# Chunked attention ahead of a routed expert layer: where the first turned queries and second turned keys are put

## The chip, the cores and the metric

The kernel runs on one core of a Trainium2 chip. The metric is device time in microseconds (us) of one execution. Before the change three executions took 534.76, 535.52 and 537.1 us, a median of 535.52 us. One more execution was taken with the hardware profiler; it is the one that all rows below come from.

The core has five engines that run side by side, each with its own queue of instructions: TensorE (PE; its weight loads are shown as PEld), VectorE (DVE), ScalarE (ACT), GpSimd (POOL) and SyncE (SP), which here only issues transfers. An engine stands at an instruction until the semaphores that it waits for have been raised; all that stands behind it on that engine waits too.

## What is computed

```python
# attention: batch 4, 8 heads, 768 tokens of 64 numbers, 8 memory keys and values per head
for c in range(S // 32):                      # chunks of 32 queries
    q_c   = q[:, :, 32*c : 32*c + 32]
    k_ctx = k[:, :, max(0, 32*c - 16) : min(S, 32*c + 40)]
    k_full, v_full = concat(mem_k, k_ctx), concat(mem_v, v_ctx)
    a = softmax(q_c @ k_full.T / 8)
    out[:, :, 32*c : 32*c + 32] = a @ v_full
# routed layer: 3072 tokens of 512 numbers, 8 experts, one expert per token
logits = x @ w_gate
e = argmax(logits);  gate = softmax(logits)[e]
y = gate * (relu(x @ w1[e]) @ w2[e])
```

All is float32. The two stages follow each other in one kernel: the attention's output rows are labelled with their expert, scattered to an array in device memory by expert, fetched back expert by expert, multiplied, and scattered to the output.

## The kernel before, in words

**Tiling of the attention.** There are 32 blocks of 96 queries (`NB`), 8 to each of the 4 batches. Two blocks in a row share one load of queries and one of keys ("super block", 16 of them, index j). `load_q(j)` and `load_k(j)` bring 384 KB each: 96 partitions, of which each holds a pair of neighbouring tokens for 8 heads. The first super block of a batch has the 8 memory keys besides (4 more partitions). `load_v(i)` brings the values of one block in three transfers into one of 6 buffers.

**Turning.** Scores need queries and keys with the 64 numbers of a head along the partitions. `turned_heads` (L616) takes one half x of the heads of a super block, issues four transposes on TensorE into one PSUM tile of 128 x 4 x 96 (or 100 with the memory keys), and returns it. `turn_q(m)` (L622) turns half x of super block j, with m = 2j + x, and copies the result out in two instructions, by default on ScalarE, into `qT`. `turn_k(m)` (L629) does this for keys, by default on VectorE, into the turned keys `kT` of the batch; with memory keys it has two more, smaller copies (L649). In what follows k0, k1, k2, ... and q0, q1, ... are these calls by their m. So k0 and k1 are the two halves of the first load of keys, k2 and k3 those of the second, k4 and k5 those of the third.

**PSUM.** Eight banks are held as three pools: `ps_s`, two pairs of banks for scores; `ps_t`, two banks for turned tiles; `ps_o`, two banks for the values. A pool's tiles take turns, so a third tile of `ps_t` waits until the first has been read.

**The order.** All is issued in the order that the code gives (`manual_schedule`). After the first nine loads come k0, k1, q0, q1 (L1038 to L1041). Then the loop over blocks i (L1042): two or more loads for later blocks; `scores(i)` (L653), four matrix products into a pair of banks and three exponentials on ScalarE into `ex`; for i = 0 alone k2 and k3 (L1048 to L1050), whose tiles come from `ps_t`; `turn_q(i + 2)`; the values of block i - 1 (L680), whose two halves are divided on VectorE; transposes and router products for earlier blocks; `turn_k(i + 4)`; routing work. A matrix product or a transpose in float32 shows as one or two records in the trace; `scores` has 8, a turn 4, `values` 16 for both halves.

The scores of block 0 read keys that k0 and k1 have turned; those of block 1 reach into keys of the second load, k2 and k3. The scores of blocks 2 and 3 need q2 and q3, and k4 and k5 besides at block 3.

**What waits for what at the start, in the code before.** q0 needs the load of queries, and the PSUM bank of k0 back, which VectorE's four copies give free; q1 needs that of k1, after ScalarE's four. The first scores need q0's copies (VectorE, L1040) and q1's (ScalarE, L1041). k2 and k3 take the two banks of `ps_t` again, VectorE copies both, and q2 and k4 take them after that.

After the attention comes the expert layer, which the change doesn't touch.

Of the kernel before, what the change touches and what calls it, by code (L numbers as in the profile page):

```python
# [10 lines left out]
F32 = mybir.dt.float32  # L11
# [8 lines left out]
B, H, S, D = 4, 8, 768, 64  # L20
# [48 lines left out]
PAIRS = QB  # L69
# [16 lines left out]
def window(qb):  # L86
    return min(max(PER * qb - LEFT, 0), KW - WIN)
# [417 lines left out]
def ordinary(ctx, tc, q, k, v, mem_k, mem_v, moe_w_gate, moe_w1, moe_w2, out, good):  # L505

    nc = tc.nc
# [7 lines left out]
    def turn(*args):  # L515
        i = nc.tensor.transpose(*args)  # L516
        cur["pe"] = i.ins.name
        return i

    def bc(ap, axis, n):  # L520
        shape = list(ap.shape)
        shape.insert(axis, n)
        idx = tuple([slice(None)] * axis + [None])
        return ap[idx].to_broadcast(shape)
# [13 lines left out]
    ps_s = actx.enter_context(tc.tile_pool(name="ps_s", bufs=2, space=PSUM))  # L538
    ps_t = actx.enter_context(tc.tile_pool(name="ps_t", bufs=2, space=PSUM))
    ps_o = actx.enter_context(tc.tile_pool(name="ps_o", bufs=2, space=PSUM))  # L540
# [47 lines left out]
    def load_runs(to, i, start, n, src, mem):  # L588

        for p, kind, r, n in runs(start, n):  # L590
            ap = (mem if kind == "mem" else src)[i // NQB, :, r : r + n].rearrange("h r d -> r h d")
            nc.sync.dma_start(to[p : p + n], ap)

    sbs = [dict() for _ in range(NSB)]
# [5 lines left out]
    def load_q(j):  # L600
        t = sbs[j]["qn"] = lpool.tile([PAIRS, H, 2 * D], F32, name="qn")
        nc.sync.dma_start(t, pairs(q, j))
        sbs[j]["qT"] = qTs[j % NQ]

    def load_k(j):
        b, s = divmod(j, NSB // B)
        t = sbs[j]["kn"] = lpool.tile([PAIRS + NMEM // 2, H, 2 * D], F32, name="kn")
        nc.sync.dma_start(t[0:PAIRS], pairs(k, j))
        if s == 0:
            nc.sync.dma_start(t[PAIRS:], mem_k[b].rearrange("h (p t) d -> p h (t d)", t=2))  # L610

    def load_v(i):
        st[i]["v"] = vs[i % NV]
        load_runs(st[i]["v"][:, :, 0:D], i, window(i % NQB), WIN, v, mem_v)

    def turned_heads(t, n, x):  # L616
        tt = ps_t.tile([128, H // 2, n], F32, tag="t", name="tqk")
        for a in range(H // 2):
            turn(tt[:, a], t[0:n, 2 * a + x], ident[0:n, 0:n])
        return tt  # L620

    def turn_q(m, copy=nc.scalar.copy):  # L622
        j, x = divmod(m, 2)
        tq = turned_heads(sbs[j]["qn"], PAIRS, x)
        to = sbs[j]["qT"][D * x : D * x + D, :, x].rearrange("d a (p t) -> d a p t", t=2)
        for t in range(2):
            copy(to[:, :, :, t], tq[D * t : D * t + D])  # L627

    def turn_k(m, copy=nc.vector.tensor_copy):  # L629
        j, x = divmod(m, 2)  # L630
        b, s = divmod(j, NSB // B)
        if s == 0 and x == 0:
            turned[b] = apool.tile([128, H // 2, KW], F32, name="kT")
        n = PAIRS + NMEM // 2 if s == 0 else PAIRS
        tk = turned_heads(sbs[j]["kn"], n, x)
        half = turned[b][D * x : D * x + D]
        for t in range(2):
            of = tk[D * t : D * t + D]
            to = half[:, :, 2 * PER * s + t : 2 * PER * s + 2 * PER]
            to = bass.AP(  # L640
                tensor=to.tensor,
                offset=to.offset,
                ap=[list(to.ap[0]), [KW, H // 2], [PER, 2], [QB // 2 + NMEM, 2], [2, QB // 4]],
            )
            i = copy(to, of[:, :, 0:PAIRS].rearrange("d a (y z p) -> d a y z p", y=2, z=2))  # L645
            keyed.setdefault((b, s), []).append(i.ins.name)
            if s == 0:
                to = half.rearrange("d a (y c) -> d a y c", y=NQB)[:, :, :, QB // 2 : QB // 2 + NMEM]
                copy(  # L649
                    to.rearrange("d a y (p t) -> d a y p t", t=2)[:, :, :, :, t], bc(of[:, :, PAIRS:], 2, NQB)  # L650
                )
# [177 lines left out]
    def routing(n, kinds="v"):  # L829
        while work and n and work[0][0] in kinds:  # L830
            kind, f = work.pop(0)
            f()
            n -= kind != "s"

    def hold_back():

        while work and work[0][0] == "s":
            spread.append(work.pop(0)[1])

    def scatter_some(n):  # L840
        while spread and n:
            spread.pop(0)()
            n -= 1

    def need(i, f, *lists):
        if 0 <= i < NB:
            f(i)
# [180 lines left out]
    with tc.manual_schedule():  # L1028
        load_k(0)
        load_q(0)  # L1030
        load_k(1)
        load_q(1)
        load_v(0)
        load_k(2)
        load_v(1)
        load_q(2)
        load_v(2)
        turn_k(0)  # L1038
        turn_k(1, nc.scalar.copy)
        turn_q(0, nc.vector.tensor_copy)  # L1040
        turn_q(1)  # L1041
        for i in range(NB):  # L1042
            if i // 2 + 3 < NSB:
                (load_k, load_q)[i % 2](i // 2 + 3)
            need(i + 3, load_v)
            scores(i)
            scatter_some(1)
            if i == 0:  # L1048
                turn_k(2)
                turn_k(3)  # L1050
            need(i + 2, turn_q)
            banks = [ps_o.tile([128, 512], F32, tag="o", name="o") for _ in range(2)]
            cur["bank"] = banks[0]
            if i <= 23:
                routing(1, "p")
            if i >= 1:
                values(i - 1, 0, banks[0])
            routing(5 if i > 23 else 3)
            need(i - 2, turn_xb)
            late = logits(i - 3, banks[1]) if i >= 3 else None  # L1060
            if i >= 1:
                values(i - 1, 1, banks[1])
            if late:
                nc.vector.tensor_copy(*late)
            if i > 23:
                routing(1, "p")
            scatter_some(1)
            need(i + 4, turn_k)
            routing(6 if i > 23 else 5)
            hold_back()  # L1070
            for g in range(len(GROUPS)):
                if i - 3 == GROUPS[g][1] - 1:
                    work.extend(routed(g))
            if i == 24:
                fetch_w(0, 4)
            if i >= 24:
                fetch_piece(1)
                fetch_piece(1)
            if len(scatters) >= EARLY and "early" not in cur:
                cur["early"] = i  # L1080
                early_count(banks[0])
                early_gather()

        early_rows()
        n = NB

        def bank_pair():
            banks = [ps_o.tile([128, 512], F32, tag="o", name="o") for _ in range(2)]
            cur["bank"] = banks[0]
            return banks  # L1090

        room_for_x()
        banks = bank_pair()
        values(n - 1, 0, banks[0])
        scatter_some(1)
        turn_xb(n - 2)
        late = logits(n - 3, banks[1])
        values(n - 1, 1, banks[1])  # L1100
        scatter_some(1)
        nc.vector.tensor_copy(*late)
        routing(99, "v")
        fetch_w(1, 1)
        fetch_piece(99)
        do_early(1)
        banks = bank_pair()
        late = logits(n - 2, banks[1])
        nc.vector.tensor_copy(*late)
        do_early(1)  # L1110
        turn_xb(n - 1)
        scatter_some(1)
        do_early(1)
        routing(1, "p")
        routing(99, "v")
        hold_back()
        banks = bank_pair()
        late = logits(n - 1, banks[1])
        nc.vector.tensor_copy(*late)
        work.extend(routed(len(GROUPS) - 1))  # L1120
        routing(99)
        check_sums()
        do_early(2)
        scatter_some(1)
        routing(1, "p")
        routing(99, "v")
        hold_back()
        do_early(1)
        scatter_some(1)
        count_up()  # L1130
        fetch_x(0)
        first_sums()
        while spread:
            do_early(1)
            scatter_some(1)
        index = [nc.tensor.value_load(cases[0:1, e : e + 1], min_val=0, max_val=len(ARMS) - 1) for e in range(E)]
        rv = nc.values_load(good[0:1, 0:1], min_val=0, max_val=1)
        tc.switch_hint({mybir.EngineType.PE: index[0]}, len(ARMS), "expert0")
        nc.tensor.addr_align(PAGE, 0, 0)
        do_early(len(early_ops))  # L1140
# [470 lines left out]
```

## Time and profile before

| | us |
|---|---|
| median of three executions | 535.52 |
| the profiled execution | 532.34 |
| its span, first to last instruction | 530.6 |
| TensorE busy within the span | 507.7 |
| VectorE busy | 300.0 |
| ScalarE busy | 245.7 |
| GpSimd busy | 156.0 |

The rows of a profile's group list give a line of the code, the engine, the operation, out<-in by the names of tiles, the count, the busy time and the mean of one in ns, and the idle time ahead of it with what ended most of that. The chain is the path of work that ended last, followed back from the last instruction; it can also be listed in order of time, as start, length, engine, tile, line and count. In the list of one line's instructions the three numbers are the shortest, the median and the longest duration in ns.

In the page's 40 slices TensorE is busy 90% or more in all but the first, one in the middle and the last. The transfer engines are busy 80% or more in the first twelve, at 154 to 344 GB/s. Over the first 40 us they moved 6.62 MB, at a mean of 165 GB/s.

### The profile page before, as it was taken

The page shows a single profiled execution, that of the slowest core. Times are in us where ns is not written, and L with a number is a line of the kernel's source. Part 1 is how long each engine was busy: PE and PEld are TensorE (multiplying, and loading weights), DVE is VectorE, ACT ScalarE, POOL GpSimd, SP SyncE. Part 2 cuts the span into 40 slices and gives each one's busy share as a digit, 9 for nine tenths or more (in the row PEclk, how much of TensorE's full clock was granted, in tenths as well). Part 3 has the DMA queues.
Part 4 walks back from the last instruction along what each step waited for, and adds up shares of the span by engine and source line. Part 5 has one row for each costly group of instructions (what it writes and reads, how often), then busy time and mean ns, then how long its engine had stood idle before and what let it go on. Part 6 is the DMA issues. An engine that isn't in the chain of part 4 may idle for free.

```text
span 530.6 us, 9604 instructions
## 1 busy us (share of the span) xinstructions
PE 507.7 (96%) x3666; PEld 475.7 (90%) x3666; DVE 300.0 (57%) x565; ACT 245.7 (46%) x445; POOL 156.0 (29%) x186
## 2 busy tenths in 40 slices
PE   3999999999999989999999999999999999999992
PEld 3899999999998569999999999977779999999991
DVE  3455656566555246878656557443625767864611
ACT  2466656556632136374553454344216637454311
POOL 2000131323373604354135054121312434412003
PEclk9999999999999999999999999999999999999997
DMA  9999999989982302446406335330505334200002
GB/s 171 154 171 181 182 224 200 224 201 344 303 308 73 88 15 81 172 172 229 176 15 221 96 128 208 102 134 30 195 18 199 139 125 182 81 15 13 1 1 84
DMA packets 81350, 75.02 MB, mean 141 GB/s; under 512 B 39543, under 2 KB 64375, under 8 KB 81281
## 3 DMA queue, kind: packets, MB, share of 16 engines
q1 hardware_dynamic: 71840, 54.60, 41.6%
q0 software_dynamic: 8768, 19.29, 11.0%
q8 instruction: 46, 0.75, 0.6%
q10 hardware_dynamic: 672, 0.18, 0.1%
q14 instruction: 24, 0.19, 0.1%
HBM read 66.13 MB, written 17.50 MB: 158 GB/s over the span
## 4 chain that ended last, share of the span: by engine, by line
PE 83%; issue 9%; DMA 3%; POOL 2%; ACT 1%; DVE 1%; POOLq 0%; ACTq 0%
PE sum_p L511 20%; PE sum_r L511 13%; PE sum_q L511 13%; PE o L511 11%; PE sc L511 8%; PE tqk L516 4%; PE sum_x L516 3%; PE ph L511 3%; PE py L511 3%; PE sum_q L516 2%; PE tx L516 2%; POOL out_dram L1276 2%; DMA xe<-x_dram,rows 1%; DMA x_dram<-xr,dest 1%; DMA kn<-in_k_dram 1%
## 5 line engine op out<-in xcount | busy, mean ns | idle before, releaser
L1276 POOL DMA_INDIRECT out_dram<-y,xe x42 | 51.0, 1214 | 177.1 <-PE sum_q L511 59.9
L1293 POOL DMA_INDIRECT xe<-x_dram,rows x35 | 50.7, 1448 | 49.8 <-PE sum_r L511 29.2
L676 ACT ACTIVATE ex<-sc,cst 128x256 f32<-128x256 f32 x96 | 38.5, 472 | 56.5 <-PE sc L511 56.5
L511 PE MATMUL o<-v,ex 128*96 128x65 f32 x512 | 54.5, 251 | 0.0
L1227 ACT COPY sum_r<-sum_p 128x640 f32<-128x640 f32 x48 | 32.5, 677 | 47.3 <-PE sum_p L511 47.2
L511 PE MATMUL sc<-qT,kT 128*128 128x192 f32 x256 | 50.6, 343 | 1.1 <-ACT qT L627 1.1
L511 PEld LDWEIGHTS o<-v,ex 128*96 128x96 f32 x512 | 49.4, 167 | 0.0
L511 PE MATMUL sum_p<-xsT,w 128*128 128x136 f32 (+6 forms) x256 | 47.6, 329 | 0.5
L511 PE MATMUL sum_r<-t,w 128*128 128x136 f32 (+6 forms) x256 | 45.8, 326 | 0.0
L511 PE MATMUL sum_p<-t,s 128*128 128x136 f32 (+6 forms) x256 | 45.6, 326 | 0.0
L801 POOL DMA_INDIRECT x_dram<-xr,dest x32 | 30.2, 944 | 52.5 <-PE tqk L516 21.3
L511 PE MATMUL sum_q<-t,s 128*128 128x136 f32 (+6 forms) x256 | 45.1, 324 | 0.0
L511 PEld LDWEIGHTS sc<-qT,kT 128*128 128x128 f32 x256 | 43.2, 199 | 1.4 <-issue 1.4
L511 PEld LDWEIGHTS sum_p<-xsT,w 128*128 128x128 f32 x256 | 39.7, 190 | 4.8 <-issue 2.1
L511 PE MATMUL sum_p<-h,w 128*128 128x136 f32 (+6 forms) x256 | 43.8, 324 | 0.0
L511 PEld LDWEIGHTS sum_p<-t,s 128*128 128x128 f32 x256 | 39.7, 190 | 2.6
L511 PEld LDWEIGHTS sum_r<-t,w 128*128 128x128 f32 x256 | 39.6, 190 | 2.6
L511 PEld LDWEIGHTS sum_q<-t,s 128*128 128x128 f32 x256 | 39.8, 190 | 2.3
L511 PEld LDWEIGHTS sum_p<-h,w 128*128 128x128 f32 x256 | 39.5, 190 | 2.3
L1224 DVE TENSOR_TENSOR h<-sum_p,kept 128x640 f32<-128x640 f32 x16 | 13.2, 824 | 48.4 <-ACT sum_r L1227 48.4
L645 DVE COPY kT<-tqk 64x384 f32<-64x384 f32 x62 | 34.3, 554 | 10.4 <-PE tqk L516 9.8
L690 DVE RECIPROCAL inv_all<-o 96x4 f32<-96x4 f32 x64 | 11.4, 179 | 48.0 <-PE o L511 47.7
(154 smaller groups left out, 916.9 us busy)
## 6 DMA issues: line engine op xcount, KB each, us to landing
w<-in_moe_w_dram SPq DMA_DIRECT2D x14, 2048.0 KB, 8.6
kn<-in_k_dram SPq DMA_DIRECT2D x16, 384.0 KB
qn<-in_q_dram SPq DMA_DIRECT2D x16, 384.0 KB
w<-in_moe_w_dram SPq DMA_DIRECT2D x8, 512.0 KB
v<-in_v_dram SPq DMA_DIRECT2D x24, 128.0 KB
v<-in_v_dram SPq DMA_DIRECT2D x24, 112.0 KB
v<-in_v_dram SPq DMA_DIRECT2D x8, 144.0 KB
v<-in_v_dram SPq DMA_DIRECT2D x8, 96.0 KB
```

The lines of the kernel that those rows point to most:

```text
L511: i = nc.tensor.matmul(*args, **more)
L516: i = nc.tensor.transpose(*args)
L645: i = copy(to, of[:, :, 0:PAIRS].rearrange("d a (y z p) -> d a y z p", y=2, z=2))
L676: nc.scalar.activation(ex4[:, :, :, sl], sc4[:, :, :, sl], AF.Exp, bias=mask[:, 3 * x + g : 3 * x + g + 1], scale=D**-0.5)
L690: nc.vector.reciprocal(inv, o[:, :, D])
L801: i = nc.gpsimd.indirect_dma_start(out=x_dram, out_offset=bass.IndirectOffsetOnAxis(ap=dest[:, t : t + 1], axis=0), in_=xr[:, t % NXR].bit ...
L1224: op(eng, one_op(lambda: engines[eng].tensor_tensor(out, a, b, op=how)), reads, writes)
L1227: op("ACT", one_op(lambda: nc.scalar.copy(to, of)), reads, writes)
L1276: return nc.gpsimd.indirect_dma_start(out=out, out_offset=bass.IndirectOffsetOnAxis(ap=which.bitcast(I32), axis=0), in_=y, in_offset=None, ...
L1293: return nc.gpsimd.indirect_dma_start(out=x[:, g].bitcast(I32), out_offset=None, in_=x_dram, in_offset=bass.IndirectOffsetOnAxis(ap=rows[: ...
```

## The change

Two tiles are taken from `ps_o` and one pair of banks from `ps_s` before the loop. q0 and q1 are turned into the first two, k2 and k3 into the two banks of the pair. k2 and k3 stand ahead of the loop now, after q1, and so ahead of the scores of block 0; k3 is copied by ScalarE and not by VectorE.

```diff
-    def turned_heads(t, n, x):
-        tt = ps_t.tile([128, H // 2, n], F32, tag="t", name="tqk")
+    def turned_heads(t, n, x, bank=None):
+        if bank is None:
+            tt = ps_t.tile([128, H // 2, n], F32, tag="t", name="tqk")
+        else:
+            tt = bank[:, 0 : H // 2 * n].rearrange("p (a n) -> p a n", a=H // 2)
...
+        first = [ps_o.tile([128, 512], F32, tag="o", name="o") for _ in range(2)]
+        second = ps_s.tile([128, 2, 512], F32, tag="s", name="sc")
         turn_k(0)
         turn_k(1, nc.scalar.copy)
-        turn_q(0, nc.vector.tensor_copy)
-        turn_q(1)
+        turn_q(0, nc.vector.tensor_copy, first[0])
+        turn_q(1, bank=first[1])
+        turn_k(2, bank=second[:, 0])
+        turn_k(3, nc.scalar.copy, second[:, 1])
         for i in range(NB):
...
             scores(i)
             scatter_some(1)
-            if i == 0:
-                turn_k(2)
-                turn_k(3)
             need(i + 2, turn_q)
```

`turn_q` and `turn_k` take the argument `bank` and hand it on to `turned_heads`.

More of the change, by code (lines that the diff above doesn't have):

```diff
@@ L620, in turned_heads, with turn_q @@
         return tt
-    def turn_q(m, copy=nc.scalar.copy):
+    def turn_q(m, copy=nc.scalar.copy, bank=None):
         j, x = divmod(m, 2)
-        tq = turned_heads(sbs[j]["qn"], PAIRS, x)
+        tq = turned_heads(sbs[j]["qn"], PAIRS, x, bank)
         to = sbs[j]["qT"][D * x : D * x + D, :, x].rearrange("d a (p t) -> d a p t", t=2)
@@ L627, in turn_q, with turn_k @@
             copy(to[:, :, :, t], tq[D * t : D * t + D])
-    def turn_k(m, copy=nc.vector.tensor_copy):
+    def turn_k(m, copy=nc.vector.tensor_copy, bank=None):
         j, x = divmod(m, 2)
@@ L634, in turn_k @@
         n = PAIRS + NMEM // 2 if s == 0 else PAIRS
-        tk = turned_heads(sbs[j]["kn"], n, x)
+        tk = turned_heads(sbs[j]["kn"], n, x, bank)
         half = turned[b][D * x : D * x + D]
```

## The prediction

> **What bounds the kernel now.** First the page's share of busy time and its chain of waits, which say that TensorE sets the end:
>
> ```profile
> PE 507.7 (96%) x3666; PEld 475.7 (90%) x3666; DVE 300.0 (57%) x565; ACT 245.7 (46%) x445; POOL 156.0 (29%) x186
> PE 83%; issue 9%; DMA 3%; POOL 2%; ACT 1%; DVE 1%; POOLq 0%; ACTq 0%
> ```
>
> So the change is worth what it does to TensorE's own line of work. That line has holes only at the start, so next the chain in order of time (start, length, what):
>
> ```profile
> 0.74 5.27 DMA kn<-in_k_dram
> ...
> 6.11 0.92 PE tqk L516 x4
> ...
> 8.68 1.53 PE tqk L516 x8
> ...
> 11.32 2.90 PE sc L511 x8
> 14.22 0.65 PE tqk L516 x4
> ...
> 16.05 0.55 DVE kT L645
> ...
> 16.61 0.57 DVE kT L645
> ...
> 17.28 0.87 PE tqk L516 x4
> 18.15 2.61 PE sc L511 x8
> ```
>
> From the first load TensorE turns k0 and k1, stands until 8.68, turns q0 and q1, stands until 11.32 for ScalarE's copies of q1, does the first scores, turns k2 and k3 (14.01 to 15.50), and then follows VectorE, whose four copies of k2 and k3 end at 17.18 and give free the banks of q2 (16.12) and of k4 (17.28). The second scores start at 17.94. From there TensorE has no hole until 27.08: third scores 23.61, one block each 4.35 us from 27.35 on.
>
> Third, the same instruction before and after some 22.75 us (four rows of lists by line: shortest, median, longest ns):
>
> ```profile
> L516 PE MATMUL tqk<-cst,kn x8: 367/367/368, 14.0 to 15.1; 96*128 96x96 f32 x8
> L511 PE MATMUL sc<-qT,kT x8: 527/527/581, 17.9 to 20.2; 128*128 128x192 f32 x8
> L511 PE MATMUL sc<-qT,kT x8: 326/326/355, 27.7 to 28.9; 128*128 128x192 f32 x8
> L516 PE MATMUL tqk<-cst,kn x8: 246/246/303, 23.3 to 27.7; 96*128 96x96 f32 x8
> ```
>
> Starts of the score records are 0.32 us apart before and 0.16 after, those of turns 0.16 and 0.08: TensorE runs at half its pace until 22.75, though the column of granted clock says 1.00 there. All of the change lies in the slow part.
>
> Fourth, when the loads land, by the trace's landing records: first keys 6.02, first queries 8.04, second keys 9.89, second queries 11.97, third keys 16.67, fourth keys 25.16. The load engines are saturated in this time (share 1.1 to 1.3 in each stretch of the first 40 us), and the change moves no load and no wait ahead of one that is late: the two loads that now wait for another turn (that of the second queries' successor, that of the second keys') are issued at over 21 us, long after those turns.
>
> **The change part by part.** What TensorE does is the same in count: no transpose, product or byte is added. VectorE gives two copies of 0.56 to ScalarE (0.50 each by its rows for k1, L645). What moves is waits.
>
> 1. q0 no longer needs k0's bank. Before, it went at 8.68, 0.09 after VectorE's last copy of k0 (8.59). Now its load is the bound: 8.04, plus the 0.09 that k0 needed after its own (6.02 to 6.11): 8.13, so 0.55 earlier. q0's copies start 0.91 later as before (8.68 to 9.59): 9.04 to 10.18 on VectorE. q1's on ScalarE start 1.55 after the first turn: 9.68 to 10.70 (1.02 for both, gap included).
> 2. k2 stands next: its load lands at 9.89, so 9.98 to 10.64 on TensorE (4 x 0.16). VectorE copies it 0.91 after the start, 10.89 to 12.01 (2 x 0.56).
> 3. k3 should follow at once. In the program built from the change it does not: its first transpose waits for VectorE's count, and the count it waits for is raised by the second copy of k2, though the two lie in two banks; they are one tile. So it goes at 12.01 + 0.09 = 12.10, done at 12.75. Queued behind it on TensorE are the first scores, which were ready at 10.79 (q1's copies). They start at 12.75 and not at 11.32: 1.43 late. Behind those, the exponentials of block 0 on ScalarE wait. ScalarE copies k3 in the hole ahead of them: 13.0 to 14.0.
> 4. After the first scores (2.69 from start to start of the next): 15.44. q2's turn has a free bank and its load: 15.44 to 16.08. k4 needs no copy now, its bank is long free, but the third keys land at 16.67: 16.76 to 17.42. Second scores: k3's copies 14.0, fine; they start at 17.42, against 17.94.
> 5. So the sum up to the second scores is -0.52 us: k2's and k3's copies (17.18) are taken off, and the third load of keys (16.67) takes their place. The 1.43 of step 3 costs nothing, because the hole ahead of 16.76 (0.68 of it) covers it; without that hole the second scores would be bound by 12.75 + 2.69 + 0.64 + 0.66 = 16.74, still earlier than before.
> 6. What is late next: the exponentials of block 0 go from 14.25 to 15.70, end 16.90, then q2's copies (1.0) until 17.9. Values of block 0 come at 20.67, q3's turn at 20.02 (needs q2's bank, 17.9): 3.8 and 2.1 us of cover. At 27.08 TensorE waits 0.27 for ScalarE's q copies, in step with the third scores, so this moves along. The fourth keys (25.16) have 2.2 of cover at 27.35.
>
> What the 0.52 are worth at the end depends on the moment when the pace doubles. If that stays at 22.75, TensorE has done 0.52 us of slow work more by then, which is 0.26 at full pace. If it moves along with the unbroken work (before: 17.28 to 22.75), it is 0.52. Ends of this unknown: -0.26 and -0.52; I take the middle, -0.4.
>
> [...]
>
> **The sum.** Profiled execution: 532.34 - 0.4 = 531.9 (span 530.2 of 530.6). The median of the runs is 3.2 above the profiled one; the same step on it: 535.52 - 0.4 = 535.1. That is 0.07%, and I call up to 0.5% (2.7 us) no change, about what a measurement of this kernel can tell: its three executions lie 2.3 apart.
>
> **The rivals.**
>
> *Full pace comes earlier, and this is worth more.* The stretch 12.10 to 16.08 has no hole now: 3.98 us. If that alone doubles the pace, from about 16: k4 16.76 to 17.10, second scores to 18.43, q3 18.77, values of block 0 to 20.1, third scores after ScalarE's q3 copies (exponentials 18.5 to 19.7, copies to 20.7) at 20.8 against 23.61: -2.8. Then the turn of the fourth keys would be due at 24.5, and they land at 25.16: only 27.35 - 25.25 = 2.1 is kept. 535.5 - 2.1 = 533.4. For it: the stretch is long. Against: before, 11.32 to 15.50 was longer (4.18) and did not do it. Loads cap it below 0.5%, so only with the spread of executions on top is it over the bound.
>
> [...]
>
> *The change doesn't do what it says: nothing is won.* Step 3 shows half of this: turns into the pair run one after the other. If the third keys land 0.5 later than in the profiled execution, k4 goes at 17.28 as before: 535.5.
>
> **How the numbers follow.** Forecast (0.1 to 0.5 us won) 0.60: 535.1, its own range 533.6 to 536.7 by the spread of the three executions. Nothing won 0.18: 535.5. Earlier full pace 0.13: 533.4. Later full pace 0.09: 539.5. The range goes from 532.6 (earlier pace, with some spread) to 537.6; beyond it lie most of the last case and tails of the others, under 2 in 10. Faster by over 0.5% (under 532.8): 0.16, half of the earlier pace and the low tail of the executions, of which the profiled one was already at 532.3. Slower by over 0.5% (over 538.2): 0.14, the later pace and the high tail. The rest, 0.70, within.
>
> **What would show it.** In the changed profile: q0's first transpose near 8.1; k3's behind a wait for VectorE's copy of k2, near 12.1; first scores near 12.75, later than before; k4's turn released by the third keys' landing near 16.75; second scores near 17.4. Wrong would be: k3 right behind k2 (step 3); a hole between 19.4 and 22.8 (slower rival); matrix products of 326 ns before 20 us (faster rival); or blocks after 30 us that no longer take 4.35, which no step of mine explains.

## The result, and the profile after

Twelve executions of the changed kernel gave a median of 536.36 us (532.67 to 538.51), twelve of the kernel before, run beside them, 536.40 (534.76 to 538.88). The ratio on record for the two sets, 0.9988, isn't that of the two medians (0.9999); its 95% interval is 0.9967 to 1.0009. By that interval the change is worth somewhere between 0.33% won and 0.09% lost: no difference that can be told. The forecast was 0.07% won.

The profiled execution after is the longer of the two profiles, 535.20 us with a span of 533.4, against 532.34 and 530.6. Its page:

```profile
span 533.4 us, 9602 instructions
...
PE 508.4 (95%) x3666; PEld 475.9 (89%) x3666; DVE 299.1 (56%) x563; ACT 246.5 (46%) x447; POOL 155.7 (29%) x186
...
PEclk9999999999988999999999999999999999999998
```

TensorE's work is the same 3666 records. What is new are the two 8s of the clock row, in the slices from 147 to 173 us (13.3 us each): TensorE ran for a while at half pace there.

The start, from the timeline (start, length, engine, line, operation, out<-in, count; in brackets the idle time ahead and what ended it):

```profile
8.22 1.54 PE L516 MATMUL o<-cst,qn 96*128 96x96 f32 x8 [0.58 <-DMA qn<-in_q_dram]
...
10.24 0.90 PE L516 MATMUL sc<-cst,kn 96*128 96x96 f32 x4 [0.48 <-DMA kn<-in_k_dram]
11.18 1.12 DVE L648 COPY kT<-sc 64x384 f32<-64x384 f32 x2 [0.90 <-PE sc L516]
...
12.36 0.90 PE L516 MATMUL sc<-cst,kn 96*128 96x96 f32 x4 [1.22 <-DVE kT L648]
...
13.06 2.82 PE L511 MATMUL sc<-qT,kT 128*128 128x192 f32 x8
...
15.67 0.79 PE L516 MATMUL tqk<-cst,qn 96*128 96x96 f32 x4
...
16.90 0.52 PE L516 MATMUL tqk<-cst,kn 96*128 96x96 f32 x4 [0.44 <-DMA kn<-in_k_dram]
...
17.26 1.49 PE L511 MATMUL sc<-qT,kT 128*128 128x192 f32 x8
```

The rows go q0 and q1, k2, its copies, k3, first scores, q2, k4, second scores. q0 is now released by its load, k3 by VectorE's copies of k2 (1.22 us of hole), k4 by the third keys. The second scores took 2.82 at their place before and take 1.49 here: in this execution the pace doubled at 16.27 by the trace's clock records, and not at 22.78. In all four profiles of kernels that keep the old start it doubled at 20.68 to 23.06; in the eight with the change or a part of it, and without products of ones at the start, it first did so at 13.76 to 20.45.

The chain in order of time shows what this ran into:

```profile
7.78 8.99 DMA kn<-in_k_dram
16.77 0.14 issue
16.90 0.33 PE tqk L516 x2
17.23 8.34 DMA kn<-in_k_dram
25.57 0.14 issue
25.71 0.52 PE tqk L516 x4
26.23 1.33 PE sc L511 x8
```

Two loads of keys in a row carry the chain from 7.78 to 25.57. TensorE waits 1.08 us for the second of them and then turns it at 25.71, 1.64 ahead of the 27.35 of the kernel before. From the same record counted along TensorE in both traces: it is 1.53 us ahead at 76 us and 1.81 ahead at 153. Then the lead is gone within one row. Before:

```profile
155.14 0.87 PE L511 MATMUL o<-v,ex 128*96 128x65 f32 x8
156.57 0.66 PE L516 MATMUL tx<-cst,xe 128*128 128x128 f32 x4 [0.56 <-DMA xe<-x_dram,rows]
...
158.99 1.99 PE L511 MATMUL ph<-x0T,w 128*128 128x256 f32 x8 [0.34 <-ACT x0T L993]
```

After:

```profile
153.12 0.39 PE L516 MATMUL tx<-cst,xr 96*128 96x96 f32 x2 [0.51 <-DVE xr L695]
...
153.96 0.87 PE L511 MATMUL o<-v,ex 128*96 128x65 f32 x8
156.48 1.12 PE L516 MATMUL tx<-cst,xe 128*128 128x128 f32 x4 [1.64 <-DMA xe<-x_dram,rows]
...
160.35 3.31 PE L511 MATMUL ph<-x0T,w 128*128 128x256 f32 x8
```

The row at 155.14 and 153.96 ends the attention's values. The next is the turn of the early rows: 256 rows of expert 0 that are fetched while the attention still runs. It starts at 156.5 in both, since its gather (the transfer that fetches these rows) lands then, at 156.52 and 156.43 by the chains, before and after:

```profile
150.16 6.36 DMA xe<-x_dram,rows
...
149.52 6.91 DMA xe<-x_dram,rows
```

The lead makes a hole of 1.64 us there and not 0.56, and one of 0.51 just ahead, at a turn of attention rows that waits for VectorE. Half pace follows (products of 128 x 256 take 3.31 us for 8 and not 1.99), by the clock column of these stretches (length, busy time and count of TensorE, granted clock, share of the transfer engines, GB/s), after:

```profile
156.40:160.00 3.60, 3.52 (x20) 0.50 0.63 209
160.00:163.00 3.00, 2.96 (x8) 0.50 0.11 38
163.00:166.00 3.00, 3.00 (x22) 0.99 0.00 0
```

The records say half pace from 156.22 to 163.04, 6.83 us. After it TensorE is 2.67 us behind the kernel before, and stays 2.7 behind to the end.

### The profile page after: what moved, and what is told of

Same layout as the page of the kernel before. It is cut to its first block, busy times and chain, and to the rows that moved or that the text cites. A ratio compares the mean times of both kernels' runs of the same rounds, so it can differ in the third digit from the quotient of the medians.

```text
span 533.4 us, 9602 instructions
## 1 busy us (share of the span) xinstructions
PE 508.4 (95%) x3666; PEld 475.9 (89%) x3666; DVE 299.1 (56%) x563; ACT 246.5 (46%) x447; POOL 155.7 (29%) x186
## 4 chain that ended last, share of the span: by engine, by line
PE 82%; issue 9%; DMA 5%; POOL 2%; SPq 1%; ACT 0%; POOLq 0%
PE sum_p L511 20%; PE sum_r L511 13%; PE sum_q L511 13%; PE o L511 11%; PE sc L511 7%; PE tqk L516 3%; PE sum_x L516 3%; DMA kn<-in_k_dram 3%; PE ph L511 3%; PE py L511 3%; PE sum_q L516 2%; PE tx L516 2%; POOL out_dram L1281 2%; DMA xe<-x_dram,rows 1%; SPq L592 1%
## 5 line engine op out<-in xcount | busy, mean ns | idle before, releaser
L511 PE MATMUL sc<-qT,kT 128*128 128x192 f32 x256 | 49.3, 337 | 0.3 <-ACT qT L630 0.3
L511 PEld LDWEIGHTS sc<-qT,kT 128*128 128x128 f32 x256 | 42.1, 195 | 0.5 <-ACT qT L630 0.5
L648 DVE COPY kT<-tqk 64x384 f32<-64x384 f32 x58 | 32.1, 554 | 11.1 <-PE tqk L516 10.5
```

Of the source, the lines that this page charges most:

```text
L511: i = nc.tensor.matmul(*args, **more)
```

## The experiments

**What the parts do at the start.** Four kernels, one profiled execution each; the kernel before took 535.74 beside them.

*k2 and k3 without the shared tile.*

```diff
-        second = ps_s.tile([128, 2, 512], F32, tag="s", name="sc")
...
-        turn_k(2, bank=second[:, 0])
-        turn_k(3, nc.scalar.copy, second[:, 1])
+        turn_k(2)
+        turn_k(3, nc.scalar.copy)
```

> The changed kernel, but k2 and k3 go to the two banks of ps_t and not to one pair of banks. Theory (the shared tile makes k3 wait, and the third load of keys sets the second scores): k3 follows k2 without a hole, near 10.9; the first scores start near 11.4 and not at 13.06; but k4's turn still starts at the landing of the third keys, 16.7 to 16.9, and the second scores within 0.3 us of the 17.26 of the changed kernel. Rival (the wait of k3 costs time that reaches the end): k4's turn and the second scores move forward too, by about 1.2 us.

Measured, TensorE's rows from k2 on:

```profile
10.52 1.51 PE L516 MATMUL tqk<-cst,kn 96*128 96x96 f32 x8 [0.44 <-DMA kn<-in_k_dram]
11.83 2.73 PE L511 MATMUL sc<-qT,kT 128*128 128x192 f32 x8
14.39 0.49 PE L516 MATMUL tqk<-cst,qn 96*128 96x96 f32 x4
17.35 0.52 PE L516 MATMUL tqk<-cst,kn 96*128 96x96 f32 x4 [2.46 <-DMA kn<-in_k_dram]
17.70 2.77 PE L511 MATMUL sc<-qT,kT 128*128 128x192 f32 x8
```

k3 follows k2 without a hole, and the first scores move from 13.06 to 11.83. All of it is given back ahead of k4, whose load landed at 17.21 here (16.77 in the profile of the changed kernel): second scores 17.70, 0.44 later, of which the landing makes 0.44. So the wait on the shared tile cost 1.2 us that nobody needed, as the theory had it. The wait for the load became one hole of 2.46 us, and the pace, which had doubled at 14.33, fell to half again from 17.74 to 21.16. The execution took 542.08 us, with five windows of half pace from 157.7 on; more on that below.

*The queries alone.* The change without its part for k2 and k3, which stay in the loop on VectorE.

> q0 and q1 go to the banks of the values; k2 and k3 stand behind the first scores and are copied by VectorE, as before the change. Theory (before the change VectorE's copies of k2 and k3 set the second scores): first scores near 11.0 (q1's copies), k2 and k3 13.6 to 15.0, VectorE's copies until 16.8, so k4's turn is released by them or by the third keys within 0.2 us of each other, and the second scores start at 17.4 to 17.6: the queries alone give most of the local gain of 0.5 to 0.7 us. Rival (the gain comes from the keys' place and ScalarE's share): second scores at 17.9 as before the change.

```profile
10.76 2.90 PE L511 MATMUL sc<-qT,kT 128*128 128x192 f32 x8 [1.13 <-ACT qT L630]
13.46 0.98 PE L516 MATMUL tqk<-cst,kn 96*128 96x96 f32 x8
15.37 0.52 PE L516 MATMUL tqk<-cst,qn 96*128 96x96 f32 x4 [0.93 <-PE tqk L516]
16.64 0.52 PE L516 MATMUL tqk<-cst,kn 96*128 96x96 f32 x4 [0.76 <-DMA kn<-in_k_dram]
17.01 2.65 PE L511 MATMUL sc<-qT,kT 128*128 128x192 f32 x8
```

k4 is released by the third keys (landing 16.51) and not by VectorE any more, and the second scores start at 17.01: the queries' part alone takes TensorE to the gate. That is sooner than expected (17.4 to 17.6), since the pace had doubled at 13.76 and k2 and k3 were turned at full pace. It fell again at 17.18. The time was 535.36.

*The keys alone.* k2 and k3 as in the change, q0 and q1 in the turned banks as before.

> k2 and k3 go ahead of the first scores into the pair, ScalarE copies k3; q0 and q1 stay in ps_t. Theory: q0 starts at 8.6 to 8.7 as before, q1's turn ends at 10.2, k2 10.3, its copies until 12.3, k3 12.4, first scores 13.1; hidden by the third keys all the same: k4's turn at 16.7 to 16.9, second scores 17.2 to 17.5, as in the changed kernel. Rival (the queries' banks matter): second scores 0.4 us or more later than in the changed kernel.

q0 starts at 8.76, k3 at 12.56, k4 at 17.16 behind a landing at 17.03, second scores 17.52 (a little over the range given; counted from the landing, 0.49, the same as the changed kernel's 0.49). The keys' part alone gets to the same gate. 535.04 us. So in these two executions either half of the change was enough to reach the gate.

*The third keys sooner.* In the changed kernel `load_k(2)` stands ahead of `load_v(0)`.

> The changed kernel with the third load of keys issued ahead of the first values. Theory (its landing is the gate): it lands at 14.3 to 15.2; k4's turn follows q2's without a hole, 16.1 to 16.5 (half pace), and the second scores start at 16.6 to 17.0 where the pace is half until then. Rival (something else releases k4): second scores at 17.2 or later.

```profile
15.86 0.85 PE L516 MATMUL tqk<-cst,qn 96*128 96x96 f32 x4
16.50 0.85 PE L516 MATMUL tqk<-cst,kn 96*128 96x96 f32 x4
17.14 1.56 PE L511 MATMUL sc<-qT,kT 128*128 128x192 f32 x8
```

The hole ahead of k4 is gone. The second scores come at 17.14, not quite as early as expected, since the loads of this execution landed 0.2 later than the changed kernel's and all ahead of it moved with them. The lead at 40 us is 2.52, the largest of all. Yet 536.78 us.

**What becomes of a lead.** At 40 us the changed kernel and these four lead the first profile by 0.7 to 2.5 us, and none of them has a gain at the end. Beside the next four kernels the kernel before gave 535.07 (531.89 to 537.99, 29 executions).

*The kernel before, profiled once more.*

> The kernel before, one more execution with the profiler. Theory (the end is set by how many windows of 3.41 us TensorE spends at half pace after a hole near 155 us, each 1.7 us): the first profile of it, with none, was the exception; this one shows a fall between 153 and 160 us, and its span is about 530.6 + 1.7 x windows, 532 to 536. Rival (the fall belongs to the change): full pace from the start's doubling to the end, span 530 to 531.

534.82 us, span 533.0: the hole ahead of the early rows was 1.14 us this time, and one window at half pace followed (159.60 to 163.01). The fall of the pace is no property of the change, and the first profile, without one, was lucky in that.

*Kept busy.* Into the changed kernel and into the kernel before go products of ones whose result nobody reads, in the two holes:

```diff
+        keep_busy(4)          # products of 128 x 128 ones, into a bank of ps_s
         turn_xb(n - 2)
...
         fetch_piece(99)
+        keep_busy(7)
         do_early(1)
```

> The changed kernel with products of ones whose result nobody reads in TensorE's two holes at 152 to 157 us (4 and 7 of them, 0.2 us each). Theory (the fall costs 1.7 us a window, most executions have two or three): no fall, span 530 to 531.5, device time 531.8 to 533.3, 0.6 to 0.9% under the kernel before. Rival (the fall costs nothing, the path goes by the transfers): time within 0.2% of the changed kernel, or 1 us more for the added products.

> The kernel before with the same added products. Theory (what the change wins at the start is lost again where the turn of the early rows waits for its gather, at 156.4 to 156.6 with and without the change): no fall, and device time within 0.6 us of the changed kernel with the same products. Rival (the win at the start is kept once the fall is gone): 1.3 us or more above it.

Changed and kept busy:

```profile
153.10 1.11 PE L1107 MATMUL idle<-ones 128*128 128x128 f32 x8
...
155.71 1.78 PE L1107 MATMUL idle<-ones 128*128 128x128 f32 x14
157.33 0.60 PE L516 MATMUL tx<-cst,xe 128*128 128x128 f32 x4
```

In the two profiles the pace no longer falls at this place: the mean granted clock is 0.992 to 0.996 in all 24 executions of the two kernels, where it was 0.985 to 0.995 in those of the changed kernel. But the time fell by much less than expected: 534.00 us for the changed kernel, 0.9993 of the kernel before (0.9967 to 1.0018), and 533.84 for the kernel before, 0.9978 (0.9954 to 1.0002). The expectation of 0.6 to 0.9% is missed. The rows say why in part: the added products themselves hold TensorE until 157.33, so the early rows start 0.85 later than 156.48. The executions still lie between 531.46 and 538.41, no closer together than those of the kernel before beside them, so the fall alone doesn't make that spread; what else does is open. The medians came out within 0.16 of each other, but this doesn't test whether a lead gets past the early rows: the added products, and not the gather, set their start here (157.33 and 157.68), and the 0.35 us between the two profiles at 153 us is 0.30 at the end.

*Warm from the start.* 11 products of ones ahead of k0 and 4 more up to k3, besides those above.

> As the changed kernel kept busy, with 11 products of ones ahead of the first turn, and 4 in the holes up to k3: TensorE has work from 1.1 us on. Theory: full pace by 4.5 to 9 us; the second scores still start only after the third keys, 17.0 to 17.3, the turn of the fourth keys after their landing at 25 to 26, 1.2 to 2.2 us ahead of the kernel before at 100 us; lost at 156.5; end as the kept busy one, within 0.5 us. Rival (a faster start is worth its time at the end): 1 us or more under the kept busy one.

Full pace from 6.39 us, and the first scores at 12.33, 0.7 earlier than in the changed kernel. Then a hole of 2.90 us until the third keys, in which the pace fell again (16.63 to 20.05), second scores at 17.74, a lead of 0.85 at 40 us (less than expected, through that fall), early rows at 157.81, 534.16 us, ratio 0.9983 (0.9962 to 1.0004). In this run a faster TensorE at the start bought nothing behind this load.

**Where the lead ends.** The first gather of the early rows takes 6.36 us from issue to landing in the first profile and 6.91 in the changed kernel's, while the transfer engines, with the two 2 MB loads of expert 1's weights among their work, move 368 and 390 GB/s on average (148 to 156 us). These weights aren't used before 200 us. In the next two kernels they wait for the second gather to land:

```diff
         fetch_w(1, 1)
-        fetch_piece(99)
+        while pieces:
+            tc.add_manual_dep(pieces.pop(0)().ins, early_gathers[-1], ...)
```

> The changed kernel; the two 2 MB loads of expert 1's weights (not needed before 200 us) wait until the second gather of the early rows has landed. Theory (in all profiles so far the turn of the early rows starts at 156.5 to 157.8, when its gather lands behind those loads, whatever lead TensorE had; and the end is that moment plus what the fall of the pace costs): the gather lands 3 to 4.5 us after its issue and not 6 to 7, the turn of the early rows follows the values at 154.5 to 155.5, no fall of the pace or one window, the lead of the start reaches the end; device time 530.5 to 532.5, 0.5 to 0.9% under the kernel before. Rival (those loads only move and cost elsewhere, or the gather is slow by itself): turn at 156.4 or later, time within 0.3% of the changed kernel.

> The kernel before with the same two loads held back. Theory: turn of the early rows right behind the values, at 156.0 to 156.6, no wait; and now the change shows at the end: 0.5 to 1.8 us slower than the changed kernel with the loads held back. Rival (the win at the start is lost in the loads of the attention itself): within 0.4 us of it.

Issue and landing of the gathers in the list of transfers, in the kernel before as it was:

```profile
xe<-x_dram,rows POOLq DMA_INDIRECT x2, 6.0
```

and in the changed kernel with the weights later, with the rows of that place:

```profile
xe<-x_dram,rows POOLq DMA_INDIRECT x2, 3.6
```

```profile
153.69 1.00 SPq L976 DMA_DIRECT2D w<-in_moe_w_dram  x2
```

```profile
154.06 0.87 PE L511 MATMUL o<-v,ex 128*96 128x65 f32 x8
154.77 0.61 PE L516 MATMUL tx<-cst,xe 128*128 128x128 f32 x4
```

And the kernel before with the weights later:

```profile
155.87 0.87 PE L511 MATMUL o<-v,ex 128*96 128x65 f32 x8
156.57 0.61 PE L516 MATMUL tx<-cst,xe 128*128 128x128 f32 x4
```

3.6 us and not 6.0 (the last figure, a median of the two gathers), the loads go out at 153.69 and not at 139, and in both kernels the early rows are turned right behind the values, with no hole and no fall. The changed kernel takes 530.71 us, 0.9938 of the kernel before on that chip (0.9912 to 0.9963), the kernel before 531.85, 0.9949 (0.9922 to 0.9977). The intervals of both lie below 1, so each is faster than the kernel before. In the two profiles the lead now reaches the end: the changed kernel is 1.08 ahead of the first profile at 153 us and 1.53 at the end, the kernel before 0.73 behind and 0.23 behind, so that 1.81 us between the two at 153 us is 1.76 at the end. The 1.1 us between their medians lie in the range expected for the theory; the two intervals overlap, so by the times it isn't settled that the change wins anything here.

*Both loads moved.* The last kernel adds the third keys ahead of the first values.

> The changed kernel with expert 1's weights held back and the third load of keys ahead of the first values. Theory (two loads are the next bounds, one at 16.7 us, one at 156 us): k4's turn behind q2's without a wait, lead at 40 us 2.0 to 2.6 us, early rows turned right behind the values, no fall of the pace; 0.3 to 1.0 us under the changed kernel with the weights alone held back, 530.0 on the same chip. Rival (loads later in the attention take the lead back): lead lost between 40 and 120 us, time within 0.3 us of it.

530.00 us, 0.9905 (0.9881 to 0.9930), the fastest, by an amount over the one above that the intervals don't separate. In its profile the rival is right: a lead of 1.80 at 76 us is 0.36 at 116. Its chain, in order of time:

```profile
67.58 6.21 DMA x_dram<-xr,dest
73.88 0.42 DVE xr L695
...
94.20 7.53 DMA x_dram<-xr,dest
101.83 0.42 DVE xr L695
```

Here scatters of finished rows take 6 to 8 us to land, VectorE waits to write their buffer again, and TensorE waits for VectorE. The attention has more places where a lead ends: five other profiles lose between 0.28 and 2.41 us from 76 to 116 us, most of all the second keys in turned banks.

**All profiles in one table.** How the same record stands at 153 us and at the end against the first profile (minus is ahead); start of the early rows' turn; windows (steps of 3.41 us) at half pace between 153 and 180 us.

| kernel | at 153 us | early rows | windows | at the end |
|---|---|---|---|---|
| before | 0 | 156.57 | 0 | 0 |
| before, again | +0.24 | 157.38 | 1 | +2.36 |
| changed | -1.81 | 156.48 | 2 | +2.70 |
| second keys in turned banks | +1.69 | 159.40 | 5 | +9.87 |
| queries alone | -1.83 | 156.47 | 3 | +3.12 |
| keys alone | -0.64 | 157.69 | 1 | +2.77 |
| third keys sooner | -1.75 | 156.50 | 3 | +3.20 |
| changed, kept busy | -0.98 | 157.33 | 0 | +0.85 |
| before, kept busy | -0.63 | 157.68 | 0 | +1.15 |
| warm and kept busy | -1.13 | 157.81 | 0 | +1.29 |
| changed, weights later | -1.08 | 154.77 | 0 | -1.53 |
| before, weights later | +0.73 | 156.57 | 0 | +0.23 |
| both loads moved | -0.36 | 155.49 | 0 | -0.80 |

The end is the start of the early rows plus the fall: take (early rows - 156.57) from the last column, and 0.04 to 0.28 is left without a fall, 1.55 and 1.65 with one window, 2.8 with two, 3.2 and 3.3 with three, 7.0 with five. The lead at 153 us enters only through the start of the early rows.

Not every lead ends at the gather itself. With the queries alone the rows are:

```profile
153.63 0.54 PE L516 MATMUL tx<-cst,xr 96*128 96x96 f32 x2 [1.04 <-DVE xr L695]
...
156.47 1.06 PE L516 MATMUL tx<-cst,xe 128*128 128x128 f32 x4
```

Here the hole ahead of the fall is the wait for VectorE. The pace falls at 153.71, and the early rows follow the values with no hole, at the same 156.5 as elsewhere. The third keys sooner show the same with a hole of 0.96 and a fall at 153.80, and the second keys in turned banks with 0.94 and 157.69. So with the queries alone and the third keys sooner the lead is spent on half pace before TensorE asks for the gather.

## Why the prediction was right, and where it was not

**Steps 1 to 4 held.** q0 8.13 foreseen, 8.22 measured; k2 9.98, 10.24; k3 12.10, 12.36; first scores 12.75, 13.06; q2 15.44, 15.67; k4 16.76, 16.90. The difference is that of the loads' landings (8.18, 10.20, 16.77). That k3 would wait for k2's copies, that the first scores would be late, and that this would cost nothing at the second scores, behind the third keys, are each shown, the last by taking the wait away (second scores no sooner).

**Step 5, the size at the second scores.** Foreseen -0.52, measured -0.68, since k4 was turned at full pace. The pair kept busy gives it at one pace: the doubling came at 20.45 with the change and 20.68 without, the second scores at 17.59 and 18.09, the turn of the fourth keys at 26.53 and 27.01. That is 0.50 and 0.48 for the change, in one pair of executions and with the doubling 0.23 apart; most of the 1.64 us in the profiled execution came with the earlier doubling.

**The pace.** The forecast put its doubling at 22.75 or 0.5 earlier; it came at 16.27, which was the rival "full pace comes earlier". What that rival said of the consequence held: third scores foreseen at 20.8, measured 21.08; the fourth keys as the cap, foreseen at 25.25 with 2.1 kept, measured 25.71 with 1.64. Its argument against itself (before, a longer stretch had not done it) didn't hold in the changed kernel: 4.18 us without a hole (11.32 to 15.50) left the pace at half in the first profile, and in the changed kernel's the pace doubled behind 3.91 (12.36 to 16.27). What set the two apart was not shown. In both profiles TensorE was busy all through the last 3.41 us ahead of the doubling (19.37 to 22.78 and 12.86 to 16.27); with the queries alone it was busy for 88% of them (10.35 to 13.76).

**The step that failed is the last one of the sum,** "what the 0.52 are worth at the end": -0.26 to -0.52 was carried to the end with no look at the place where TensorE next waits for something other than its own work. It rests on the sentence that TensorE's line "has holes only at the start", which the first profile itself contradicts: 0.56 us ahead of 156.57, behind the gather. In the profiled pair the lead, though larger than forecast, is lost there: 1.81 us at 153 us, 0.09 at the early rows. That the forecast came out right is luck in part: what it forecast, 0.07%, is too small to tell from nothing, and no difference that can be told arrived. The times can't say whether all of the 0.5 us is lost on average; the interval would allow a win of 0.33%. The rival "the change doesn't do what it says: nothing is won" had the outcome right with a wrong place: not the third keys, but 156 us.

**The base was off as well.** The prediction took the profiled execution, 532.34, as an ordinary one with the median 3.2 above it. It was one without a fall of the pace at 156 us; all six other profiles of kernels that kept the attention's end as it was (the changed one, its four variants, the kernel before again) have one to five windows of half pace there. The three executions on record then, 534.76 to 537.1, were all slower than the profiled one, and nothing on record gave their clock.

**The later full pace,** with 0.09 at 539.5, adds 4.35 us for one block more at half pace, and no run shows that term. A hole between 19.4 and 22.8 came in the changed kernel, 0.32 us ahead of the third scores at 21.08, behind ScalarE's copies of queries; but the pace was full by then and stayed so. What the runs showed in its place are falls of one step at the start of three other kernels (17.74 to 21.16 with the second keys in turned banks, for one), and half pace at the other end of the attention, in both kernels: 6.83 us in the changed kernel's profile, 3.41 in the second one of the kernel before.

## What to carry to other kernels

A win early in a kernel is followed to the next place where the busy engine waits for a transfer with its own timetable; if there is one, the win can be lost there until that is moved. Look there first: here two loads that nobody needed for 50 us took a small gather that the path needed at once from 3.6 to 6.0 us, and holding them back gave 0.5 to 0.6% where the change alone gave nothing that could be told. And one profile is one execution: before an execution is taken as the base, compare its clock row with the mean granted clock of the others.

## What the runs showed of the chip

TensorE's pace changed in steps of 3.413 us: full from 22.78 to 524.54 us in the first profile is 147.0 of them, and the falls lasted 3.41, 6.83, 10.24 and 17.07. The phase differed between executions: the first doublings of the first profile (22.78) and of the changed kernel's (16.27) lie 6.51 us apart, 1.91 steps. Over all profiles the first doubling came between 6.39 (with products of ones from 1.06 on) and 23.06.

What changes the pace doesn't come out of these runs. With turns and products counted alike, two steps of nearly the same busy share ended differently: in the first profile the step from 12.54 to 15.95 (counted back from 22.78) was 87% busy, and half pace went on behind it (43% of the step products, 44% turns); in the kernel with the queries alone the step from 10.35 to 13.76 was 88% busy (79% products, 9% turns), and the pace doubled behind it. A step of nothing but turns (254.89 to 258.30 in the first profile) had full pace behind it.

The busy share doesn't tell the falls apart either. Half pace came behind a step with 1.69 of 3.41 us idle (152.81 to 156.22 in the changed kernel), and full pace stayed behind one with as much idle time (185.92 to 189.34 in the changed kernel with the weights later). Half pace came behind one that was 72% busy (150.39 to 153.80, third keys sooner), and full pace stayed behind one that was 63% busy (186.62 to 190.03 in the first profile). And with the second keys in turned banks half pace stayed behind two steps full of products (164.52 to 171.34). What set these apart is open.

A small gather took longer beside large loads: 6.0 us (median of two) in the kernel before, beside two loads of 2 MB, and 3.5 with these held back.
